# Splitting the contraction of a feed-forward: 128 rows at once, or two halves of 64 rows into two PSUM banks

## The chip, the cores and the metric

The kernel runs on one core of a Trainium2 chip. A core has a matrix engine (TensorE, PE in the profile) that reads both operands from SBUF and writes only to PSUM, three engines for elementwise work (VectorE or DVE, ScalarE or ACT, GpSimd or POOL), and a queue (SyncE or SP) from which this kernel issues its DMAs. PSUM has eight banks; one bank holds 128 partitions of 512 float32 values. The metric is the device time of one execution, in microseconds (us); lower is better. A profiled execution gives a trace of every instruction, and the profile's times count from the first instruction (the span).

## The reference

Block-sparse attention over 4 batches of 8 heads, 768 positions and 64 dimensions, and then a feed-forward over its output:

```python
scores = scale * np.matmul(q, k.transpose(0, 1, 3, 2))
scores = np.where(mask, scores, -1000000000.0)   # own block and its neighbours, first and last block, 3 sampled blocks
attn = np.exp(scores - np.max(scores, axis=-1, keepdims=True))
attn = attn / (np.sum(attn, axis=-1, keepdims=True) + 1e-09)
x = np.matmul(attn, v)            # (4, 8, 768, 64), then transposed to (3072 tokens, 512)
h = x @ w_in                      # (3072, 512) @ (512, 2048)
r = np.maximum(h, 0.0)
g = s * (r * r) + b               # s and b are single numbers
return (g @ w_out).astype(np.float32)   # (3072, 2048) @ (2048, 512)
```

The weights arrive as 64-bit floats. The feed-forward is kept near float32 accuracy by writing each operand as a high and a low part in the fast float32 form of TensorE (`F32R`, fp32r in the profile) and forming three of the four products: high by high, high by low, low by high.

## The kernel before

**Attention** (the first 290 us) works through 'units' of one head pair and 128 query positions. Its instructions are put in order by a planner in the kernel: each operation has an engine, an estimated cost, a due time (priority) and its dependences, and the planner simulates the engines to write an order for each queue. The table `T` holds the due times, among them those of the K loads (`KL`), the query loads (`QL`), the gathers of sampled V blocks (`GV`) and the latency assumed for the weight loads (`LATE`). The attention output goes to DRAM (`xd`) and comes back transposed for the feed-forward.

**Feed-forward.** The 3072 tokens form 8 groups of 384 tokens (`G`), the hidden dimension 16 blocks of 128. A 'sub' is one group and one block, `subs[i] = (g, f)`, 128 subs in all. Groups 0 and 1 come first, interleaved (subs 0 to 31; the planner orders the first 30 of them beside the end of the attention and the decoding of the weights). Groups 2 to 7 follow, one after the other, 16 subs each, 96 subs in all, in the order in which the loop at the end of the kernel writes them. For one sub:

- `mlp1(i)`: 4 chunks of the model dimension by 3 products = 12 matmuls, each a 128x128 weight block against 384 token columns, all summed in one PSUM bank. The banks alternate: `i % 2`.
- `relu(i)` on ACT reads that bank into SBUF, `square(i)` on DVE multiplies by itself and by `s`, `hidden_high(i)` on ACT adds `b` and rounds to the high part, `hidden_low(i)` on POOL takes the difference as the low part.
- `mlp2(i)`: 3 token tiles of 128 by 3 products = 9 matmuls, each 128x128 of the hidden values against 512 output columns, summed over all 16 blocks in one bank per token tile. Groups with even and odd number use different banks (2 to 4, and 5 to 7). At the last block (f = 15) the three banks are copied to SBUF, by ACT, DVE and ACT, and stored.

In the loop, PE's order is `mlp1(i)`, `mlp2(i-2)`, `mlp1(i+1)`, `mlp2(i-1)` and so on, so the elementwise chain of a sub has the time of three blocks of PE work between its first use and its last. Each engine runs its own queue in order and waits only on semaphores.

Attention already has matmuls that use half of the array's rows: `scores_static` (L694) multiplies 64 dimensions of one head, with `tile_position=(0, 0)` for one head and `(64, 0)` for the other, each into its own bank.

Of the kernel before, what the change touches and what calls it, by code (L numbers as in the profile page):

```python
# [14 lines left out]
AF = mybir.ActivationFunctionType  # L15
ALU = mybir.AluOpType
# [3 lines left out]
P = 128  # L20
# [182 lines left out]
def kernel(  # L203
# [176 lines left out]

    def mlp1(i, cs=range(NCC)):
        g, f = subs[i]
        if 0 in cs:
            hid[i] = bank(i % 2, f"h{g}_{f}")[:, :G]
        ph = hid[i]
        for c in cs:
            xh, xl = (xsp[(g, k)][:, c, :] for k in range(2))
            wh, wl = (win(f, k)[:, c * P:(c + 1) * P] for k in range(2))
            nc.tensor.matmul(ph, wh, xh, start=(c == 0), stop=False)  # L389
            nc.tensor.matmul(ph, wh, xl, start=False, stop=False)  # L390
            nc.tensor.matmul(ph, wl, xh, start=False, stop=(c == NCC - 1))  # L391

    def relu(i):
        nc.scalar.activation(htile(i % 2), hid.pop(i), AF.Relu)  # L394

    def square(i):
        t = htile(i % 2)
        nc.vector.scalar_tensor_tensor(out=t, in0=t, scalar=sb_s, in1=t, op0=ALU.mult, op1=ALU.mult)  # L398

    def hidden_high(i):  # L400
        t, gh = htile(i % 2), htile(2 + i % 3)
        nc.scalar.activation(t, t, AF.Identity, bias=sb_b)  # L402
        nc.scalar.copy(gh, t)  # L403
# [11 lines left out]
    def mlp2(i):  # L415
        g, f = subs[i]
        gh, gl = htile(2 + i % 3), htile(5 + i % 3)
        b, hf = divmod(g, 2)
        for t in range(TG):
            if f == 0:  # L420
                po[(g, t)] = bank(2 + 3 * hf + t, f"o{g}_{t}")
            acc = po[(g, t)]
            tsl = slice(t * P, (t + 1) * P)
            nc.tensor.matmul(acc, gh[:, tsl], wout(f, 0), start=(f == 0), stop=False)  # L424
            nc.tensor.matmul(acc, gh[:, tsl], wout(f, 1), start=False, stop=False)  # L425
            nc.tensor.matmul(acc, gl[:, tsl], wout(f, 0), start=False, stop=(f == NFC - 1))  # L426
            if f == NFC - 1:
                ob = wos["pool"].tile([P, DM], F32, tag="ob", name=f"ob{g}_{t}", bufs=3)
                if t % 2 == 0:
                    nc.scalar.copy(ob, acc)  # L430
                else:
                    nc.vector.tensor_copy(ob, acc)
                tok = BLK + hf * G + t * P
                if tok + P <= S:
                    nc.sync.dma_start(out=out[b * S + tok:b * S + tok + P, :], in_=ob)
                else:
                    nc.sync.dma_start(out=out[b * S + tok:(b + 1) * S, :], in_=ob[:P - BLK])
                    nc.sync.dma_start(out=out[b * S:b * S + BLK, :], in_=ob[P - BLK:])
# [4 lines left out]
    with ExitStack() as es:  # L443
# [498 lines left out]
        for i, (kind, b, t, x) in enumerate(slots):  # L942
# [3 lines left out]
            if qk not in lqs:  # L946
                for par in range(2):
                    pq = lqs[qk] = op("s", 450, u - (T["QL"] if i else 50) + 0.1 * par, lambda qk=qk, par=par: load_q(qk, par), alloc=[] if par else [("qr", qk)],
# [99 lines left out]
        for k, (which, f) in enumerate((w[0], int(w[1:])) for w in T["WL"].split()):  # L1048
# [3 lines left out]
            mine = {}  # L1052
            for m, (eng, fn, needs) in enumerate(st):
# [62 lines left out]
    for i in range(NPL, NSUB + LAG):  # L1116
        s = SUB0 + i
        if i < NSUB:
            mlp1(i)
        if i - LAG >= NPL - 1:  # L1120
            mlp2(i - LAG)
        if i < NSUB:
            relu(i)
# [86 lines left out]
```

## Time and profile before

| | |
|---|---|
| time, median of 3 runs | 828.12 us (822.63 to 832.83) |
| profiled execution | 827.27 us, its span 825.5 us |
| PE busy | 803.8 us of the span, 97% |
| PE's granted clock, mean | 0.993 |
| ACT, DVE, POOL busy | 57%, 49%, 25% |

The table of the profile's first part gives each engine's busy time. 'PEld' is the loading of weights into the array, which has its own record for every matmul. A PE record lasts from its start to a modelled end that includes the pipeline's latency, so consecutive records overlap: what a matmul costs in a dense stream is the distance from one start to the next, not its duration. The timeline gives the start and length in microseconds, then engine, line, operation, what is written and read, and the shape (weights first for a matmul, as rows*columns, then the moving operand).

### The profile page before, as it was taken

The numbers are of one execution on the slowest core, as the hardware profiler recorded it, in microseconds if no ns is written. First come the engines' busy times: TensorE is split into PE (matmuls) and PEld (weight loads), VectorE is DVE, ScalarE is ACT, GpSimd is POOL, SyncE is SP. The second block draws the span as 40 slices with busy tenths as digits, with TensorE's granted clock in tenths as the row PEclk, the third lists the DMA queues.
The fourth block names the chain that finished last, engine by engine and source line by source line (L and its number), as shares of the span: only waits on it lengthen the run. The fifth ranks groups of instructions, "written<-read, shape, count | busy, mean of one in ns | idle before, by whom it ended". The sixth has DMA issues, their size and how long they took to land.

```text
span 825.5 us, 21605 instructions
## 1 busy us (share of the span) xinstructions
PE 803.8 (97%) x8512; PEld 699.8 (85%) x8512; DVE 408.0 (49%) x1061; ACT 472.9 (57%) x1107; POOL 206.8 (25%) x436
## 2 busy tenths in 40 slices
PE   7889999999999999999999999999999999999998
PEld 5677877888876889999989999999999999999996
DVE  4666778888987899999631221212212112122111
ACT  3666768878886788778554434434434444444433
POOL 1722133222300032222222222222222222222221
PEclk9999999999999999999999999999999999999999
DMA  8997897877777423433130010002002002001001
GB/s 253 271 234 279 225 254 199 246 234 226 213 198 225 142 102 102 129 107 123 39 115 1 1 66 11 1 1 77 0 1 77 1 1 77 0 1 39 1 1 38
DMA packets 79061, 89.03 MB, mean 108 GB/s; under 512 B 10736, under 2 KB 57968, under 8 KB 78960
## 3 DMA queue, kind: packets, MB, share of 16 engines
q1 hardware_dynamic: 78960, 87.66, 36.3%
q8 instruction: 67, 1.10, 0.6%
q14 instruction: 34, 0.28, 0.1%
HBM read 75.05 MB, written 12.58 MB: 106 GB/s over the span
## 4 chain that ended last, share of the span: by engine, by line
PE 88%; DMA 4%; SPq 3%; issue 2%; DVE 1%; ACT 1%; POOL 0%; DVEq 0%; POOLq 0%; ACTq 0%
PE o L425 11%; PE o L426 11%; PE o L424 11%; PE h L391 10%; PE h L389 10%; PE h L390 10%; PE t L771 8%; PE xs L816 5%; PE s L694 4%; PE xs L830 3%; PE s L720 2%; DMA kt<-in_k_seq_dram 2%; PE s L708 1%; DMA vg<-in_v_dram 1%; SPq L637 1%
## 5 line engine op out<-in xcount | busy, mean ns | idle before, releaser
L407 POOL TENSOR_TENSOR hid<-hid,hid 128x384 fp32r<-128x384 f32 x128 | 135.2, 1057 | 465.9 <-ACT hid L403 456.4
L398 DVE SCALAR_TENSOR_TENSOR hid<-hid,sb_s 128x384 f32<-128x384 f32 x128 | 83.3, 652 | 306.0 <-ACT hid L394 305.8
L389 PE MATMUL h<-x,win 128*128 128x384 f32 x512 | 172.7, 337 | 0.6 <-ACT hid L394 0.6
L391 PE MATMUL h<-x,win 128*128 128x384 f32 x512 | 172.7, 337 | 0.0
L390 PE MATMUL h<-x,win 128*128 128x384 f32 x512 | 172.1, 336 | 0.2 <-DVE x L363 0.2
L394 ACT ACTIVATE hid<-h 128x384 f32<-128x384 f32 x128 | 62.7, 490 | 153.7 <-PE h L391 152.1
L747 ACT ACTIVATE ptile<-ptile,nm 128x352 f32<-128x352 f32 (+2 forms) x208 | 120.8, 583 | 32.5 <-DVE nm L735 31.6
L402 ACT ACTIVATE hid<-hid,sb_b 128x384 f32<-128x384 f32 x128 | 78.8, 616 | 72.9 <-DVE hid L398 72.9
L389 PEld LDWEIGHTS h<-x,win 128*128 128x128 f32 x512 | 96.2, 188 | 6.5 <-ACT hid L394 0.9
L390 PEld LDWEIGHTS h<-x,win 128*128 128x128 f32 x512 | 96.1, 188 | 5.8 <-DVE x L363 0.6
L391 PEld LDWEIGHTS h<-x,win 128*128 128x128 f32 x512 | 96.0, 188 | 0.0
L654 POOL COPY kg<-kt 128x128 f32 x264 | 63.6, 293 | 128.0 <-PE s L720 123.9
L735 DVE CUSTOM_DVE_ANT_0 ptile<-s,ms 128x352 f32<-128x352 f32 x160 | 74.4, 521 | 27.3 <-PE s L720 27.0
L771 PE MATMUL t<-ident,ptile 128*128 128x128 f32 x608 | 79.7, 280 | 1.7 <-DVE nm L735 0.9
L426 PE MATMUL o<-wout,hid 128*128 128x512 f32 x192 | 75.9, 395 | 0.0
L426 PE MATMUL o<-woutr,hid 128*128 128x512 f32 x192 | 75.9, 395 | 0.0
L425 PE MATMUL o<-wout,hid 128*128 128x512 f32 x192 | 75.8, 395 | 0.0
L425 PE MATMUL o<-woutr,hid 128*128 128x512 f32 x192 | 75.8, 395 | 0.0
L424 PE MATMUL o<-wout,hid 128*128 128x512 f32 x192 | 74.7, 389 | 0.0
L424 PE MATMUL o<-woutr,hid 128*128 128x512 f32 x192 | 74.6, 389 | 0.0
L771 PEld LDWEIGHTS t<-ident,ptile 128*128 128x128 f32 x608 | 66.5, 142 | 7.9 <-ACT ptile L747 2.2
L403 ACT CAST hid<-hid 128x384 fp32r<-128x384 f32 x128 | 65.8, 514 | 4.4 <-PE o L425 0.4
(131 smaller groups left out, 1080.8 us busy)
## 6 DMA issues: line engine op xcount, KB each, us to landing
vg<-in_v_dram SPq DMA_DIRECT2D x136, 128.0 KB, 3.7
v<-in_v_sta_dram SPq DMA_DIRECT2D x40, 256.0 KB, 4.3
kt<-in_k_seq_dram SPq DMA_DIRECT2D x16, 544.0 KB, 7.3
raw_i<-in_w_in_dram SPq DMA_DIRECT2D x16, 512.0 KB, 4.0
raw_o<-in_w_out_dram SPq DMA_DIRECT2D x16, 512.0 KB, 3.2
v<-in_v_dram SPq DMA_DIRECT2D x16, 384.0 KB, 6.1
xd<-xst SPq DMA_DIRECT2D x44, 128.0 KB, 3.9
xraw<-xd SPq DMA_DIRECT2D x14, 384.0 KB, 4.1
```

Of the source, the lines that this page charges most:

```text
L389: nc.tensor.matmul(ph, wh, xh, start=(c == 0), stop=False)
L390: nc.tensor.matmul(ph, wh, xl, start=False, stop=False)
L391: nc.tensor.matmul(ph, wl, xh, start=False, stop=(c == NCC - 1))
L398: nc.vector.scalar_tensor_tensor(out=t, in0=t, scalar=sb_s, in1=t, op0=ALU.mult, op1=ALU.mult)
L402: nc.scalar.activation(t, t, AF.Identity, bias=sb_b)
L407: nc.gpsimd.tensor_tensor(out=htile(5 + i % 3), in0=t, in1=gh.bitcast(F32), op=ALU.subtract)
L424: nc.tensor.matmul(acc, gh[:, tsl], wout(f, 0), start=(f == 0), stop=False)
L425: nc.tensor.matmul(acc, gh[:, tsl], wout(f, 1), start=False, stop=False)
L426: nc.tensor.matmul(acc, gl[:, tsl], wout(f, 0), start=False, stop=(f == NFC - 1))
L735: nc.vector.tensor_tensor_reduce(out=pt[:, :w], in0=sps.pop((n, g))[:, :w], in1=msk, scale=-scale, scalar=FMAX if g == 0 else nm[:, 0:1], ...
L747: nc.scalar.activation(pt[:, :w], pt[:, :w], AF.Exp, bias=nms[n][:, last:last + 1], scale=-1.0, accum_out=dns[i][:, g, j:j + 1])
L771: nc.tensor.transpose(tp[:, c, :], src[:, c * P:(c + 1) * P], ident)
```

## The change

From group 2 on (`in_halves`), each matmul of `mlp1` and `mlp2` becomes two: rows 0 to 63 of both operands at tile position (0, 0) into one bank, rows 64 to 127 at (64, 0) into another. `mlp1` now fills banks 0 and 1 for every sub in place of alternating; `mlp2` holds six banks (2 to 7) for the three token tiles of a group, in place of three banks and the other three for the next group. The two sums of a hidden tile are added on the way out: ACT copies the first bank, DVE adds the second, and then DVE squares with the maximum against zero inside (`scalar=0.0`, `ALU.max`), while `s` moves into ACT's scale. The output tiles are also copied by ACT and added to by DVE. `relu(i)` is written ahead of `mlp2(i-2)` in the loop, for all subs. Subs 0 to 31 keep whole products.

In the planner's table four due times change, the first query load takes the common due time, and the load of group 0's tokens is ordered behind that of weight block i7. Instructions of PE and POOL in the attention keep their order.

```diff
-    "GK": 9.0, "GV": [7.0, 15.0, 15.0, 15.0, 15.0, 15.0], "KL": [46.0, 18.0, 26.0, 26.0], "QL": 18.0, "VL": 10.0, "SI": 31.8, "MS1": -23.3, "MS2": -1.6,
+    "GK": 9.0, "GV": [9.0, 15.0, 15.0, 15.0, 15.0, 15.0], "KL": [26.0, 18.0, 26.0, 26.0], "QL": 18.0, "VL": 10.0, "SI": 31.8, "MS1": -23.3, "MS2": -1.6,
...
+    row_halves = [slice(0, P // 2), slice(P // 2, P)]
+    def in_halves(i):
+        return subs[i][0] >= 2
+    def products(to, pairs, first, last):
+        for k, (w, x) in enumerate(pairs):
+            start, stop = first and k == 0, last and k == len(pairs) - 1
+            if len(to) == 1:
+                nc.tensor.matmul(to[0], w, x, start=start, stop=stop)
+            else:
+                for rows, o in zip(row_halves, to):
+                    nc.tensor.matmul(o, w[rows], x[rows], start=start, stop=stop, tile_position=(rows.start, 0))
     def mlp1(i, cs=range(NCC)):
-            hid[i] = bank(i % 2, f"h{g}_{f}")[:, :G]
+            hid[i] = [bank(k, f"h{g}_{f}_{k}")[:, :G] for k in ((0, 1) if in_halves(i) else (i % 2,))]
...
-            nc.tensor.matmul(ph, wh, xh, start=(c == 0), stop=False)
-            nc.tensor.matmul(ph, wh, xl, start=False, stop=False)
-            nc.tensor.matmul(ph, wl, xh, start=False, stop=(c == NCC - 1))
+            products(hid[i], [(wh, xh), (wh, xl), (wl, xh)], c == 0, c == NCC - 1)
     def relu(i):
-        nc.scalar.activation(htile(i % 2), hid.pop(i), AF.Relu)
+        h = hid.pop(i)
+        if in_halves(i):
+            t = htile(i % 2)
+            nc.scalar.copy(t, h[0])
+            nc.vector.tensor_tensor(out=t, in0=h[1], in1=t, op=ALU.add)
+        else:
+            nc.scalar.activation(htile(i % 2), h[0], AF.Relu)
     def square(i):
+        if in_halves(i):
+            nc.vector.scalar_tensor_tensor(out=t, in0=t, scalar=0.0, in1=t, op0=ALU.max, op1=ALU.mult)
     def hidden_high(i):
-        nc.scalar.activation(t, t, AF.Identity, bias=sb_b)
+        nc.scalar.activation(t, t, AF.Identity, bias=sb_b, scale=sb_s if in_halves(i) else 1.0)
     def mlp2(i):
-                po[(g, t)] = bank(2 + 3 * hf + t, f"o{g}_{t}")
+                po[(g, t)] = [bank(k, f"o{g}_{t}_{k}") for k in ((2 + 2 * t, 3 + 2 * t) if in_halves(i) else (2 + 3 * hf + t,))]
...
+                if in_halves(i):
+                    nc.scalar.copy(ob, acc[0])
+                    nc.vector.tensor_tensor(out=ob, in0=acc[1], in1=ob, op=ALU.add)
...
-                    pq = lqs[qk] = op("s", 450, u - (T["QL"] if i else 50) + 0.1 * par, lambda qk=qk, par=par: load_q(qk, par), alloc=[] if par else [("qr", qk)],
+                    pq = lqs[qk] = op("s", 450, u - T["QL"] + 0.1 * par, lambda qk=qk, par=par: load_q(qk, par), alloc=[] if par else [("qr", qk)],
...
+            if which == "i" and f == 7:
+                for c2 in range(2):
+                    xl[(0, c2)].order.append(pw)
...
             mlp1(i)
+            relu(i)
         if i - LAG >= NPL - 1:
             mlp2(i - LAG)
-        if i < NSUB:
-            relu(i)
```

PE's queue before, at the end of a sub's `mlp2` and the start of the next `mlp1` in group 3 (`o3_2` is the bank of group 3's third token tile, `h3_11` that of hidden block 11; `hid` are hidden values, `x3_0` and `x3_1` the high and low parts of the tokens, `win` and `woutr` weights):

```order
L424 MATMUL o3_2_8741<-woutr_7562,hid4_7125 128x512
L425 MATMUL o3_2_8741<-woutr_7562,hid4_7125 128x512
L426 MATMUL o3_2_8741<-woutr_7562,hid7_7139 128x512
L389 MATMUL h3_11_8978<-x3_0_8455,win2_7437 128x384
L390 MATMUL h3_11_8978<-x3_1_8457,win2_7437 128x384
L391 MATMUL h3_11_8978<-x3_0_8455,win2_7437 128x384
```

Three products of the tile are followed by the first three products of the next hidden block.

PE's queue in the changed kernel, at the same place (the last number before the buffer's own is the bank):

```order
L395 MATMUL o3_2_6_9166<-woutr_7596,hid7_7125 128x512
L395 MATMUL o3_2_7_9167<-woutr_7596,hid7_7125 128x512
L395 MATMUL h3_11_0_9590<-x3_0_8647,win2_7462 128x384
L395 MATMUL h3_11_1_9591<-x3_0_8647,win2_7462 128x384
L395 MATMUL h3_11_0_9590<-x3_1_8649,win2_7462 128x384
L395 MATMUL h3_11_1_9591<-x3_1_8649,win2_7462 128x384
L395 MATMUL h3_11_0_9590<-x3_0_8647,win2_7462 128x384
L395 MATMUL h3_11_1_9591<-x3_0_8647,win2_7462 128x384
```

Every row has become two neighbours that differ in the bank alone (`_0` and `_1`, `_6` and `_7`); the rows of one product stand next to each other.

DVE's queue before, where group 4's output is copied out while group 5 has begun (`hid0`, `hid1` are the two buffers of hidden values, `ob4_1` the copy of group 4's second token tile):

```order
L398 SCALAR_TENSOR_TENSOR hid1_7088<-hid1_7088,sb_s_62 128x384
L398 SCALAR_TENSOR_TENSOR hid0_7051<-hid0_7051,sb_s_62 128x384
L432 COPY ob4_1_9623<-o4_1_9196 128x512
L398 SCALAR_TENSOR_TENSOR hid1_7088<-hid1_7088,sb_s_62 128x384
L398 SCALAR_TENSOR_TENSOR hid0_7051<-hid0_7051,sb_s_62 128x384
```

DVE has one square per sub, and one of the group's three output copies.

DVE's queue in the changed kernel, at the same place (`h5_1_1` is the second bank of group 5's hidden block 1):

```order
L411 TENSOR_TENSOR hid0_7061<-h5_0_1_10676,hid0_7061 128x384
L418 SCALAR_TENSOR_TENSOR hid0_7061<-hid0_7061 128x384
L411 TENSOR_TENSOR hid1_7080<-h5_1_1_10726,hid1_7080 128x384
L451 TENSOR_TENSOR ob4_0_10759<-o4_0_3_9984,ob4_0_10759 128x512
L451 TENSOR_TENSOR ob4_1_10769<-o4_1_5_9992,ob4_1_10769 128x512
L451 TENSOR_TENSOR ob4_2_10779<-o4_2_7_10000,ob4_2_10779 128x512
L418 SCALAR_TENSOR_TENSOR hid1_7080<-hid1_7080 128x384
L411 TENSOR_TENSOR hid0_7061<-h5_2_1_10788,hid0_7061 128x384
```

Each square has an addition ahead of it, and three output additions stand between the addition and the square of block 1.

SP's queue at the start of the kernel before (`qr0_5d` is the first query tile, `kt0` and `kt1` the keys of batches 0 and 1, `sbi` the sampled block numbers):

```order
L484 DMA qr0_5d_160<-in_q_edge_dram 64x4x128 x2
L474 DMA kt0_168<-in_k_seq_dram 128x1088 x4
L534 DMA sbi_177<-in_sampled_dram 128x144
L474 DMA kt1_179<-in_k_seq_dram 128x1088
L484 DMA qr1_5d_181<-in_q_edge_dram 64x4x128 x2
```

SP's queue at the start of the changed kernel:

```order
L557 DMA sbi_160<-in_sampled_dram 128x144
L497 DMA kt0_162<-in_k_seq_dram 128x1088 x3
L507 DMA qr0_5d_171<-in_q_edge_dram 64x4x128 x2
L497 DMA kt0_162<-in_k_seq_dram 128x1088
L497 DMA kt1_183<-in_k_seq_dram 128x1088
L507 DMA qr1_5d_187<-in_q_edge_dram 64x4x128 x2
```

The block numbers have moved to the front, and the first query tile behind three of the four key loads. Further on, the first V gather stands ahead of the first store to `xd` in place of behind it.

More of the change, by code (lines that the diff above doesn't have):

```diff
@@ L383, in mlp1 @@
         if 0 in cs:
-            hid[i] = bank(i % 2, f"h{g}_{f}")[:, :G]
-        ph = hid[i]
+            hid[i] = [bank(k, f"h{g}_{f}_{k}")[:, :G] for k in ((0, 1) if in_halves(i) else (i % 2,))]
         for c in cs:
@@ L388, in mlp1 @@
             wh, wl = (win(f, k)[:, c * P:(c + 1) * P] for k in range(2))
-            nc.tensor.matmul(ph, wh, xh, start=(c == 0), stop=False)
-            nc.tensor.matmul(ph, wh, xl, start=False, stop=False)
-            nc.tensor.matmul(ph, wl, xh, start=False, stop=(c == NCC - 1))
+            products(hid[i], [(wh, xh), (wh, xl), (wl, xh)], c == 0, c == NCC - 1)
     def relu(i):
-        nc.scalar.activation(htile(i % 2), hid.pop(i), AF.Relu)
+        h = hid.pop(i)
[5 more added lines that the diff above has]
+            nc.scalar.activation(htile(i % 2), h[0], AF.Relu)
     def square(i):
         t = htile(i % 2)
-        nc.vector.scalar_tensor_tensor(out=t, in0=t, scalar=sb_s, in1=t, op0=ALU.mult, op1=ALU.mult)
+        if in_halves(i):
+            nc.vector.scalar_tensor_tensor(out=t, in0=t, scalar=0.0, in1=t, op0=ALU.max, op1=ALU.mult)
+        else:
+            nc.vector.scalar_tensor_tensor(out=t, in0=t, scalar=sb_s, in1=t, op0=ALU.mult, op1=ALU.mult)
     def hidden_high(i):
         t, gh = htile(i % 2), htile(2 + i % 3)
-        nc.scalar.activation(t, t, AF.Identity, bias=sb_b)
+        nc.scalar.activation(t, t, AF.Identity, bias=sb_b, scale=sb_s if in_halves(i) else 1.0)
         nc.scalar.copy(gh, t)
@@ L420, in mlp2 @@
             if f == 0:
-                po[(g, t)] = bank(2 + 3 * hf + t, f"o{g}_{t}")
+                po[(g, t)] = [bank(k, f"o{g}_{t}_{k}") for k in ((2 + 2 * t, 3 + 2 * t) if in_halves(i) else (2 + 3 * hf + t,))]
             acc = po[(g, t)]
             tsl = slice(t * P, (t + 1) * P)
-            nc.tensor.matmul(acc, gh[:, tsl], wout(f, 0), start=(f == 0), stop=False)
-            nc.tensor.matmul(acc, gh[:, tsl], wout(f, 1), start=False, stop=False)
-            nc.tensor.matmul(acc, gl[:, tsl], wout(f, 0), start=False, stop=(f == NFC - 1))
+            products(acc, [(gh[:, tsl], wout(f, 0)), (gh[:, tsl], wout(f, 1)), (gl[:, tsl], wout(f, 0))], f == 0, f == NFC - 1)
             if f == NFC - 1:
                 ob = wos["pool"].tile([P, DM], F32, tag="ob", name=f"ob{g}_{t}", bufs=3)
-                if t % 2 == 0:
-                    nc.scalar.copy(ob, acc)
+                if in_halves(i):
+                    nc.scalar.copy(ob, acc[0])
+                    nc.vector.tensor_tensor(out=ob, in0=acc[1], in1=ob, op=ALU.add)
+                elif t % 2 == 0:
+                    nc.scalar.copy(ob, acc[0])
                 else:
-                    nc.vector.tensor_copy(ob, acc)
+                    nc.vector.tensor_copy(ob, acc[0])
                 tok = BLK + hf * G + t * P
```

2 rows, old and new, of the table T are left out of this document.

## The prediction

> **What bounds the kernel now.** I read the page first, then stretches of 50 us, then single instructions.
>
> ```profile
> span 825.5 us, 21605 instructions
> PE 803.8 (97%) x8512; PEld 699.8 (85%) x8512; DVE 408.0 (49%) x1061; ACT 472.9 (57%) x1107; POOL 206.8 (25%) x436
> ...
> PE 88%; DMA 4%; SPq 3%; issue 2%; DVE 1%; ACT 1%; POOL 0%; DVEq 0%; POOLq 0%; ACTq 0%
> ```
>
> PE is busy for 97% of the span and makes 88% of the chain that ended last. The stretches say where it is alone (columns: length, busy time of PE, PEld, DVE, ACT, POOL, PE's granted clock, DMA share, GB/s).
>
> ```profile
> 0.00:50.00 50.00, 40.54 (x567) 30.12 (x568) 27.47 (x105) 25.48 (x75) 22.29 (x104) 0.96 0.97 260
> ...
> 550.00:600.00 50.00, 50.00 (x253) 45.29 (x252) 10.50 (x17) 21.95 (x42) 12.17 (x12) 1.00 0.10 32
> ```
>
> In the stretch of the changed subs PE never stops, at full clock, while DVE works a fifth of the time and ACT less than half. So only what a product costs on PE, or a new stop of PE, can move the time. One sub of the changed stretch:
>
> ```profile
> 601.68 0.39 PE L424 MATMUL o<-woutr,hid 128*128 128x512 f32 x1
> ...
> 603.76 0.33 PE L389 MATMUL h<-x,win 128*128 128x384 f32 x1
> ```
>
> ```profile
> 601.94 0.49 ACT L394 ACTIVATE hid<-h 128x384 f32<-128x384 f32 x1 [1.85 <-PE h L391]
> 602.47 0.62 DVE L398 SCALAR_TENSOR_TENSOR hid<-hid,sb_s 128x384 f32<-128x384 f32 x1 [3.10 <-ACT hid L394]
> 603.12 0.62 ACT L402 ACTIVATE hid<-hid,sb_b 128x384 f32<-128x384 f32 x1 [0.69 <-DVE hid L398]
> 603.77 0.51 ACT L403 CAST hid<-hid 128x384 fp32r<-128x384 f32 x1
> 604.41 1.02 POOL L407 TENSOR_TENSOR hid<-hid,hid 128x384 fp32r<-128x384 f32 x1 [3.17 <-ACT hid L403]
> 606.13 0.49 ACT L394 ACTIVATE hid<-h 128x384 f32<-128x384 f32 x1 [1.85 <-PE h L391]
> ```
>
> A sub takes 4.19 us (601.94 to 606.13): 2.08 for the nine products of `mlp2` (601.68 to 603.76), 2.11 for the twelve of `mlp1`. The chain from the end of `mlp1` to the low part ends at 605.43, while `mlp2` of that sub starts two subs later, near 610: it is covered by over 4 us.
>
> What is in a product? Two dense runs of one kind give its parts, before and after the mixed stretch.
>
> ```profile
> 290.72 0.33 PE L389 MATMUL h<-x,win 128*128 128x384 f32 x1
> ...
> 293.84 0.33 PE L389 MATMUL h<-x,win 128*128 128x384 f32 x1
> ...
> 817.51 0.39 PE L425 MATMUL o<-woutr,hid 128*128 128x512 f32 x1
> ...
> 820.91 0.39 PE L425 MATMUL o<-woutr,hid 128*128 128x512 f32 x1
> 821.14 0.39 PE L426 MATMUL o<-woutr,hid 128*128 128x512 f32 x1
> ```
>
> From 290.72 to 293.84 there are 18 steps: 3.12 / 18 = 0.1733 us for 384 columns. From 817.51 to 820.91 there are 15: 3.40 / 15 = 0.2267 us for 512. The difference, 0.0533 over 128 columns, is 0.417 ns per column, and what is left is fixed: 0.1733 - 384 x 0.417 ns = 13.3 ns for each product. This fixed part is 12 x 13.3 + 9 x 13.3 = 0.28 us of a sub; the rest of the 4.19 is 3.84 of streaming and 0.07 where the two kinds follow each other.
>
> **The change part by part.**
>
> *Products in halves.* A half streams as many columns as the whole product, so the pair costs one product only if the halves run side by side, and it gains only if the fixed part shrinks. The attention already has such pairs, in plain float32, 64 rows by 256 columns, each product in two passes; they run here between 154.69 and 155.82.
>
> ```profile
> 154.69 0.49 PE L694 MATMUL s<-kt,qr_0s 64*128 64x256 f32 x2
> 154.69 1.13 PE L694 MATMUL s<-kt,qr_0s 64*128 64x256 f32 x8
> L694 PE MATMUL s<-kt,qr_0s x8: 376/376/480, 154.7 to 155.5; 64*128 64x256 f32 x8
> L694 PEld LDWEIGHTS s<-kt,qr_0s x2: 183/183/183, 154.7 to 154.7; 64*128 64x128 f32 x2
> ```
>
> The first two records (x2) last 480 ns each and 0.49 us together, so both halves run at once, and so do their two weight loads, which start together at 154.7. The first pair has 104 ns of exposed load (480 against 376). The last pair starts 1.13 - 0.376 = 0.754 after the first, so three steps of a pair take 0.754 - 0.104 = 0.65, 0.217 us each. If such a pass streams a column in two of the steps found above, 256 columns take 0.213, and the pair's fixed part is 3 ns. So side by side is shown, and at this slower rate the fixed part is almost nothing. What these rows do not show is whether the fixed part is small because of the halves or because of the rate.
>
> I take the rate. The fixed part lies inside the record of a product: 0.334 - 0.160 = 0.174 us beside its columns, against 0.376 - 0.213 = 0.163 for the half-row pass. And the row at 821.14 is the kernel's last matmul; no load follows it, yet it lasts 0.39 as the others do. So it isn't the next load that stretches it, and each half streams the same columns through its own rows, with a load of its own. I put the pair at the whole product's price: 0 us for 96 subs. The bounds are 96 x 21 x (13.3 - 3) = -20.8 us, with the 0.07 at the joints -27.5 us, and the other way 13.3 ns more per pair, +26.8 us.
>
> *Additions.* DVE gets one addition per sub. Its nearest rows are the subtraction and the square, and for the output the copy:
>
> ```profile
> L398 DVE SCALAR_TENSOR_TENSOR hid<-hid,sb_s 128x384 f32<-128x384 f32 x96 | 62.6, 652 | 296.4 <-ACT hid L394 296.4
> L363 DVE TENSOR_TENSOR x<-xraw,x 128x384 fp32r<-128x384 f32 x20 | 11.0, 552 | 0.0
> L432 DVE COPY ob<-o 128x512 f32<-128x512 f32 x7 | 4.8, 691 | 28.6 <-PE o L426 26.1 <-DMA out_dram<-ob 2.5
> ```
>
> I take 0.62 for 384 elements (0.55 to 0.65) and 0.70 for 512 (0.69 to 0.76). In an ordinary sub this lies beside PE: 96 x 0.62 us on an engine that is 80% idle. The chain grows from 3.5 to 4.15 us and keeps over 3 us of cover. New is that banks 0 and 1 serve every sub: `mlp1(i+1)` waits for the addition of sub i, done 0.26 + 0.49 + 0.04 + 0.62 = 1.41 us after `mlp1(i)`; it starts after 2.08. Cover 0.67 us, cost nothing.
>
> *Group ends.* Here the cover goes. Behind the addition of sub (g+1, 1) DVE's queue holds three output additions, and behind them the square.
>
> ```profile
> 489.54 0.59 ACT L430 COPY ob<-o 128x512 f32<-128x512 f32 x1 [2.48 <-PE o L426]
> 490.92 0.59 ACT L430 COPY ob<-o 128x512 f32<-128x512 f32 x1 [0.80 <-PE o L426]
> ```
>
> Count from the end of `mlp1`, when `mlp2` begins; tile 0's third product starts 2 x 0.23 after that, lasts 0.39 and can be copied from 0.90 on; tile 2 follows 1.38 later (489.54, 490.92), tile 1 midway. ACT copies to 1.49, 2.18, 2.87; DVE adds to 2.23, 2.93, 3.63, squares to 4.25; ACT's two steps end at 5.44, and only then comes its copy of the next sub, to 5.96, and DVE's addition to 6.62. PE wants bank 1 at 4.19 + 2.08 = 6.27. It stops 0.4 us, at 5 group ends: +2.0 us (3.0 with the slower additions).
>
> *Tail.* The last output tile is copied and then added to: +0.04 + 0.70 = +0.74 us. The last low part, 0.66 later, is ready at 819.6, just ahead of its first use near 819.8; at a faster PE it would cost some tenths.
>
> *Attention.* The sampled numbers move ahead, the first query tile behind more key loads.
>
> ```profile
> 10.33 2.80 PE L708 MATMUL s<-kt,qr_5d 64*64 64x384 f32 x28
> ...
> 49.32 1.03 PE L830 MATMUL xs<-vg,pt 96*32 96x64 f32 x26 [2.18 <-DMA vg<-in_v_dram]
> ...
> kt<-in_k_seq_dram SPq DMA_DIRECT2D x16, 544.0 KB, 7.3
> ```
>
> Earlier gathers can end the wait of 2.18 us at 49.32. Against it, PE's first scores at 10.33 need the query tile, and that tile now has one key load (544 KB) ahead of it that these scores don't read; at 260 GB/s, the rate of the first stretch, that is 2.1 us. I take 0, with -2.2 and +2.1 as ends.
>
> Sum against the profiled execution: 827.27 + 0 + 2.0 + 0.74 + 0 = 830.0 us. That execution lies 0.85 us under the median of the runs shown, less than they spread (822.63 to 832.83). What a measurement of this kernel can tell from no change is about 2%: below 811.6 or above 844.7.
>
> **The rivals.**
>
> *The fixed part goes.* A load for one half could run under the other half, and the fixed part fall to the 3 ns of the attention's pairs. For it: the pair rows above. Against it: loads ride under whole products already.
>
> ```profile
> 601.16 0.33 PE L389 MATMUL h<-x,win 128*128 128x384 f32 x1
> ...
> 601.16 0.19 PEld L390 LDWEIGHTS h<-x,win 128*128 128x128 f32 x1
> ```
>
> The load for the next product starts with this one, in the same rows of the array. The Trainium skill, "TensorE: Matmul & The Clock Gate", Part 3 (packing small matmuls), says that a weight load overlaps a running matmul only where the row groups differ; by that rule whole products pay for loads that halves hide. The trace disagrees with its letter, since the loads are recorded inside the products; by it the 13.3 ns would be the unhidden rest. Time: a pair costs 0.163 and 0.216, the sub 12 x 0.163 + 9 x 0.216 = 3.90, so 96 x -0.29 = -27.8 us. The group ends then cost 0.8 each (PE wants bank 1 at 5.85), 4 us, and the tail 1 us: 804.5 us. Chance 0.28.
>
> *The fixed parts add.* Each half brings its own 13.3 ns, and one stands in the way of the other, since both leave one queue in order. For it: PE issues twice the instructions. Against it: in the 3 ns of the attention's pair there is no room for this. Place: every pair of the 96 subs; price 13.3 ns x 21 x 96 = 26.8 us; it decides, by passing 2%, from (844.7 - 830.0) / (96 x 21) = 7 ns more per pair. The slower PE hides the group ends: 827.27 + 26.8 + 0.74 = 855 us. Chance 0.17.
>
> *The halves don't run side by side.* At the fast rate a pair would hand over two columns for each one of the whole product, which no row here shows. If halves follow each other, each sub costs another 4.1 us: about 1220 us. If only the loads do, a pair of 384 waits for 2 x 104 ns: 12 x (0.208 - 0.174) x 96 = 39 us, 868 us. Together 0.09. The Trainium skill, "TensorE: Matmul & The Clock Gate", in its table of why this matters, says that a product of few rows takes as long as one of all rows and the gain lies in running tiles together; it also gives 3.07 for four such tiles. By that figure, 0.77 a tile, I estimate two halves at 1.3 products, near 950 us; no run here shows it.
>
> **How the numbers follow.** Forecast 0.46 (820 to 840 us), fixed part gone 0.28, fixed parts added 0.17, one after the other 0.09. Range: down to 800, the first rival with the gain of the attention; up to 858, the second with its loss; that leaves out the last rival and the edges. Faster by over 2%: 0.28, and 0.01 of the forecast's edge; slower: 0.17 + 0.09, with 0.01 of that edge; within 2%: 0.44.
>
> **What would show it.** Two records of one product start within 0.01 us, and from pair to pair it is 0.173 to 0.185 for 384 columns and 0.227 to 0.236 for 512: then the pair has the old price. Near 0.163 and 0.216 the first rival is right, with means above 0.183 and 0.238 (now 0.176 and 0.231) the second; a second half that starts after the first half's columns shows the third. ACT's copies at the same distance as before, 4.19 us, is the sum of it. PE's wait for DVE at five group ends, some 0.4 us each, shows the queue on DVE; none there, and the walk was wrong. The wait on `vg` near 49 and PE's first scores show the attention's part.

## The result, and the profile after

The changed kernel takes 838.72 us (median of 4, 833.08 to 841.07), beside 830.31 us for the kernel before on the same chip (median of 4, 822.63 to 832.83): a ratio of 1.0124, with a 95% interval of 1.0079 to 1.0169. It is slower by 10 us, within the 2% and inside the range. The profiled execution takes 838.24 us against a forecast of 830.0, so 8 us are unaccounted for. The ratios leave out slow executions, among them one of 978.51 us of the planner's part alone and one of 1971.61 us of the halves alone, which the medians include. The page of the changed kernel, first its span, the engines' busy time and the chain that ended last:

```profile
span 836.5 us, 25875 instructions
PE 809.4 (97%) x10528; PEld 733.9 (88%) x10528; DVE 458.7 (55%) x1169; ACT 485.4 (58%) x1113; POOL 206.9 (25%) x436
...
PE 87%; DVE 4%; DMA 3%; SPq 2%; ACT 2%; issue 1%; ACTq 0%; DVEq 0%
```

PE is busy 5.6 us longer, with a span 11 us longer: so part of the loss is PE standing still, and part is PE working more slowly. DVE works 50.7 us more and is still at 55%. The stretches of the changed kernel (the same columns as before: length, busy PE, PEld, DVE, ACT, POOL, granted clock, DMA share, GB/s):

```profile
0.00:50.00 50.00, 42.05 (x571) 32.14 (x572) 27.55 (x106) 24.81 (x74) 22.59 (x104) 0.90 0.93 248
240.00:260.00 20.00, 14.94 (x276) 12.73 (x267) 11.19 (x38) 11.43 (x35) 0.00 (x0) 0.83 0.63 183
248.60:252.00 3.40, 3.40 (x67) 3.11 (x68) 0.42 (x3) 3.16 (x10) 0.00 (x0) 0.50 0.27 48
412.00:416.00 4.00, 2.02 (x5) 1.42 (x6) 3.71 (x7) 1.28 (x4) 0.08 (x1) 0.83 0.59 195
416.00:420.00 4.00, 4.00 (x17) 3.52 (x17) 1.81 (x3) 0.70 (x2) 0.00 (x0) 0.74 0.01 4
550.00:600.00 50.00, 50.00 (x506) 49.86 (x504) 15.66 (x28) 22.47 (x41) 12.20 (x12) 1.00 0.10 33
```

The last row is the stretch that the change rewrote, and nothing is wrong there: PE full, clock full, twice the instructions (506, or 253 pairs, where 253 products stood before). The damage is in rows 2 to 5, near 245 and 415 us, in work that the halves don't touch. What PE waited for there, by its waits (total, times, longest) and then by the timeline (in brackets the idle time before an instruction, and what ended it):

```profile
PE xs L839 <- ACT xst L870: 5.1, 1, 5.1
...
PE o L392 <- DVE woutr L83: 1.7, 1, 1.7
...
PE s L731 <- DMA qr_5d<-in_q_edge_dram: 1.1, 1, 1.1
```

```profile
245.25 0.93 ACT L361 CAST x<-xraw 128x384 fp32r<-128x384 f32 x2 [6.82 <-DMA xraw<-xd]
248.58 1.98 PE L839 MATMUL xs<-v,pt 128*64 128x64 f32 x32 [5.07 <-ACT xst L870]
...
413.29 0.49 PE L392 MATMUL o<-woutr,hid 128*128 128x512 f32 x1 [1.71 <-DVE woutr L83]
414.47 3.63 PE L392 MATMUL o<-woutr,hid 128*128 128x512 f32 x8 [0.69 <-DVE woutr L85]
```

Near 243 us ACT stands for 6.82 us at the splitting of group 0's tokens, whose load is now ordered behind weight block i7 (it goes out at 240.13 us, where in the kernel before it went out at 197.78 and the splitting at 223.51 found it done); behind it in ACT's queue are the copies that PE's next matmuls need, and PE stops for 5.07 us. Near 412 us PE waits 1.71 and 0.69 us for an output weight that DVE has decoded too late. With both stops the clock falls: it is granted 0.50 over 3.4 us from 248.6 on, and 0.74 from 416 to 420.

A table of where each feed-forward product starts shows when the time is lost. It counts the 2688 products in order (a pair of halves is one), and gives the changed kernel's start less that of the kernel before, in us, from the two traces:

| place | product | after - before | gained or lost since the row above |
|---|---|---|---|
| first product of the feed-forward (286.39 and 282.34) | 0 | +4.05 | +4.05 |
| inside groups 0 and 1 | 200 | +4.83 | +0.78 |
| just ahead of the waits for the late weight | 600 | +4.83 | 0 |
| after them | 640 | +9.38 | +4.55 |
| passage from whole to half products | 714 | +10.12 | +0.74 |
| five group ends later | 2600 | +10.24 | +0.12 |
| last product | 2687 | +10.28 | +0.04 |
| end of the span (836.5 and 825.5) | | +11.0 | +0.7 |

Of the 11 us, 9.4 are lost before the first half product has run. The first row compares two single executions, and some 3 us of it belong to the execution and not to the edits (see the attention, in the part on why the prediction was right or wrong).

### The profile page after: what moved, and what is told of

It is laid out like the page before. It is cut to its first block, busy times and chain, and to the rows that moved or that the text cites. A ratio compares the mean times of both kernels' runs of the same rounds, so it can differ in the third digit from the quotient of the medians.

```text
span 836.5 us, 25875 instructions
## 1 busy us (share of the span) xinstructions
PE 809.4 (97%) x10528; PEld 733.9 (88%) x10528; DVE 458.7 (55%) x1169; ACT 485.4 (58%) x1113; POOL 206.9 (25%) x436
## 4 chain that ended last, share of the span: by engine, by line
PE 87%; DVE 4%; DMA 3%; SPq 2%; ACT 2%; issue 1%; ACTq 0%; DVEq 0%
PE o L395 24%; PE h L395 24%; PE t L794 8%; PE o L392 7%; PE h L392 6%; PE xs L839 5%; PE s L717 4%; PE xs L853 3%; PE s L743 2%; DMA kt<-in_k_seq_dram 2%; PE xs L828 1%; PE s L731 1%; PE xs L865 1%; SPq L660 1%; DMA vg<-in_v_dram 1%
## 5 line engine op out<-in xcount | busy, mean ns | idle before, releaser
L395 PE MATMUL h<-x,win 64*128 64x384 f32 x2304 | 230.9, 334 | 0.0
L395 PEld LDWEIGHTS h<-x,win 64*128 64x128 f32 x2304 | 219.9, 184 | 3.5 <-issue 0.7
L424 ACT ACTIVATE hid<-hid,sb_b,sb_s 128x384 f32<-128x384 f32 x96 | 68.0, 709 | 106.4 <-DVE hid L418 106.4
L395 PE MATMUL o<-wout,hid 64*128 64x512 f32 x864 | 114.1, 390 | 0.0
L395 PE MATMUL o<-woutr,hid 64*128 64x512 f32 x864 | 113.5, 390 | 0.0
L395 PEld LDWEIGHTS o<-woutr,hid 64*128 64x128 f32 x864 | 98.9, 184 | 2.5
L395 PEld LDWEIGHTS o<-wout,hid 64*128 64x128 f32 x864 | 98.6, 184 | 2.8
L392 PE MATMUL h<-x,win 128*128 128x384 f32 x384 | 72.3, 338 | 0.0
L392 PEld LDWEIGHTS h<-x,win 128*128 128x128 f32 x384 | 68.0, 189 | 2.7 <-DVE x L363 0.2
L798 DVE COPY pt<-t 128x384 f32<-128x384 f32 (+1 forms) x104 | 56.5, 546 | 12.8 <-PE t L794 10.7
```

Source lines behind the costliest of these rows:

```text
L392: nc.tensor.matmul(to[0], w, x, start=start, stop=stop)
L395: nc.tensor.matmul(o, w[rows], x[rows], start=start, stop=stop, tile_position=(rows.start, 0))
L424: nc.scalar.activation(t, t, AF.Identity, bias=sb_b, scale=sb_s if in_halves(i) else 1.0)
L798: nc.vector.tensor_copy(to, src)
```

## The experiments

The first question was whether the halves or the planner's five edits (three due times at the start, `LATE`, the order of the token load) cost the time. "Theory 1" in the first expectations is that the planner's edits do; from the second set on, "theory 2" names what followed from it. The intervals below are at 95%, and the us in brackets are the ratio's interval times the median of the kernel before.

**The planner's part alone.** The kernel before, whole products throughout, with the change's edits to the planner:

```diff
-"LATE": 3000.0  GV[0] 7.0  KL[0] 46.0
+"LATE": 5000.0  GV[0] 9.0  KL[0] 26.0
-u - (T["QL"] if i else 50) + 0.1 * par
+u - T["QL"] + 0.1 * par
+            if which == "i" and f == 7:
+                for c2 in range(2):
+                    xl[(0, c2)].order.append(pw)
```

> The kernel before with only the planner's part of the change: LATE 5000, first GV 9, first KL 26, the common due time for the first query load, and group 0's token load ordered behind weight block i7. Whole products throughout. Theory 1 (the time that was lost comes from the planner's part): 836 to 840 us, first matmul of the feed-forward some 4 us later than before, and a second loss of 4 to 5 us between 400 and 430 us. Rival (it comes from the halves, with their additions and the earlier reading of the first bank): 827 to 831 us, as before.

Measured 833.26 us, ratio 1.0073 (1.0038 to 1.0109): +6.0 us (3.1 to 9.0), under the 836 to 840 us that theory 1 expected of it. Both stops are there (4.9 us for `xst`, 1.7 and 0.7 for the late weight), but its attention was otherwise shorter: its first feed-forward product starts 0.93 us after that of the kernel before, and not 4.05.

**The halves alone.** The changed kernel with the diff above taken back.

> The changed kernel with the planner's part taken back: halves, additions and the earlier relu alone. Theory 1: 829 to 831 us, 1 us above before (0.6 us at the end for the additions, a few tenths at group ends). Rival (the halves cost the time): 836 to 840 us.

828.43 us, ratio 1.0006 (0.9972 to 1.004). The halves, their additions, the shared banks and the moved `relu` together make no difference that can be measured. In its trace the halves cost 0.73 us at the passage and 0.19 at the group ends, near the changed kernel's 0.74 and 0.16, and 0.6 at the end: 1.5 us, which the interval does not rule out (-2.3 to +3.3 us).

**The price of a product.** The prediction took the fixed 13.3 ns of a product to stay with halves; the Trainium skill's rule and the attention's pairs spoke for the other way. The kernel before, with dense runs added at its end that nothing interrupts (24 products each, 12 in plain float32); its time thus holds some 60 us of added work (two of the ten runs are shown; the comments say what each is):

```diff
+    for k in range(24):
+        nc.tensor.matmul(Q[0], fr[k % 2][:, :P], fr[k % 2], start=True, stop=True)          # L1148, F32R, 128 rows
...
+        for j in range(2):
+            nc.tensor.matmul(Q[j], fr[k % 2][H[j], :P], fr[k % 2][H[j]], start=True, stop=True, tile_position=(64 * j, 0))   # L1158
```

> The kernel before, with ten dense runs of matmuls behind its last one, each 24 or 12 products long, which cost extra time at the end only and whose sums nobody reads: fast float32 in whole rows with 512 and with 256 columns, with 64 in place of 128 weight columns, in quarters of 32 rows, in halves, in one half alone; plain float32 whole and in halves; bfloat16 whole and in halves. Theory A (the fixed 13.3 ns belongs to each product in the fast float32 form, whatever rows it has, and halves merely run two such chains side by side): 0.227 us from product to product for 512 columns in whole rows, in halves, in quarters and for a half alone; 0.120 for 256; plain float32 near 0.429 a pass, whole as in halves; bfloat16 near 0.216. Theory B (it belongs to any product at one column a step): bfloat16 at 0.227 too. Theory C (it is the weight load's, and grows with its columns): 0.220 with 64 weight columns, the others as in A.

The timeline of this kernel's PE, one row for each run (start, length of the whole run, number of records):

```profile
824.30 5.60 PE L1148 MATMUL bench<-woutr 128*128 128x512 f32 x24
829.74 3.03 PE L1150 MATMUL bench<-woutr 128*128 128x256 f32 x24
832.61 5.68 PE L1152 MATMUL bench<-woutr 128*64 128x512 f32 x24
838.22 5.77 PE L1155 MATMUL bench<-woutr 32*128 32x512 f32 x96
843.92 5.74 PE L1158 MATMUL bench<-woutr 64*128 64x512 f32 x48
849.50 5.60 PE L1160 MATMUL bench<-woutr 64*128 64x512 f32 x24
855.03 10.57 PE L1162 MATMUL bench<-woutr 128*128 128x512 f32 x24
865.52 10.57 PE L1165 MATMUL bench<-woutr 64*128 64x512 f32 x48
876.25 5.13 PE L1167 MATMUL bench<-benchw 128*128 128x512 bf16 x23 [0.16 <-issue]
881.31 5.35 PE L1170 MATMUL bench<-benchw 64*128 64x512 bf16 x48
```

A run's length less one record (0.39 us in F32R, 0.60 in plain float32, 0.38 in bf16, 0.28 for 256 columns), over its steps, is the price. F32R: whole 5.21 / 23 = 0.227 us; one half alone the same (L1160); pairs of halves 0.233 and quarters 0.234, and without their first step (0.335 and 0.340 us from the first start to the second) 0.228 as well. 64 in place of 128 weight columns (L1152): 0.230, no cheaper. 256 columns: 2.75 / 23 = 0.120. Plain float32, two passes and records a product: 0.434 a pass with the first step, 0.429 by the starts of the others, whole or halved, so 2 x 213.3 + 2.6 ns. bf16: 4.75 / 22 (one record is missing) = 0.216 whole, 0.216 halved, 2.5 ns over its columns. Theory B falls with the bf16 runs, and theory C with the 64 weight columns. Theory A holds: the 13.3 ns belong to the F32R product, whatever rows it uses, and the 3 ns of the attention's pairs belong to plain float32 and not to halves. The Trainium skill, "TensorE: Matmul & The Clock Gate", Part 1 ("Wait — 56ns, not 53.3ns?"), gives about 2.5 ns over the columns for a bf16 matmul at full clock; the bf16 runs here agree (215.8 ns, 2.5), and F32R pays five times that. The rule of Part 3 of the same page of the Trainium skill that was weighed in the prediction, loads overlap only where row groups differ, would have made halves cheaper: they take 0.228 against 0.227.

**`LATE` and the order without the start's numbers.**

```diff
-"LATE": 3000.0
+"LATE": 5000.0
+            if which == "i" and f == 7:
+                for c2 in range(2):
+                    xl[(0, c2)].order.append(pw)
```

> The kernel before with two pieces of the planner's part that bear on the weights: LATE 5000 and group 0's token load behind weight block i7. Theory 1a (these two make the stops near 243 and 411 us, where ACT waits for the tokens and PE for late weights): 833 to 838 us with a wait of some 5 us of PE near 243. Rival 1b (the order at the start makes the difference, by shifting what comes later): 827 to 831 us, and no such wait.

837.26 us, ratio 1.0113 (1.0054 to 1.0173): +9.4 us (4.5 to 14.3). PE's wait near 243 is 5.6 us, its first feed-forward product comes 4.70 us late, and the waits for the weight add 4.5: these two edits alone give the whole loss, and the three others must gain. That gave the next set, one edit each.

**The start's numbers alone** (`GV[0]`, `KL[0]`, the first query load):

```diff
-GV[0] 7.0  KL[0] 46.0   u - (T["QL"] if i else 50) + 0.1 * par
+GV[0] 9.0  KL[0] 26.0   u - T["QL"] + 0.1 * par
```

> The kernel before with three of the planner's changes alone: the gather's due time GV[0] 9, the key load's KL[0] 26, and the first query load on the common due time. Theory 2 (the planner's part is three pieces that add up): these numbers save 3 to 3.6 us of the attention by 100 us, as in the two runs that had them (the changed kernel -3.15, the planner's part alone -3.57), nothing stops PE near 243 or 411 us, and the gain stays to the end: 1 to 4 us under the kernel before. Rival 2b (the gain is lost again, since the end of the attention waits for transfers that don't come earlier): PE is ahead at 100 us and level again at the first feed-forward product, no difference.

820.97 us, ratio 0.9957 (0.9924 to 0.999): -3.6 us (-6.3 to -0.8), faster than both kernels. By its windows PE is busy for 43.37 us of the first 50, where it was 40.54:

```profile
0.00:50.00 50.00, 43.37 (x579) 33.15 (x580) 28.52 (x107) 25.39 (x76) 22.42 (x104) 0.90 0.93 250
```

The wait for `vg` near 49 us is gone, and PE is 3.9 us ahead near 71 us. It stays ahead, by 3.3 us near 237 us and by 6.2 at the first feed-forward product of this execution: rival 2b falls. A single trace says little here, since the attention varies from one execution to the next; but near 86 us PE is 2.7 to 3.6 us ahead in all five traces with the start's numbers, and in the six others it lies between 1.5 us ahead of the kernel before and 3.0 behind it.

**`LATE` alone.**

> The kernel before with LATE 5000 alone. Theory 2: no wait near 243; DVE takes hidden squares ahead of pieces of the last output weight's decoding, and near 411 us PE waits 1.7 and 0.7 us for that weight and then goes at half clock for a while: +4 to +5 us in all. Rival 2a (the late decoding comes from the order of the token load, which also moves DVE's and ACT's queues): within 1 us of the kernel before, no wait for the weight.

831.09 us, ratio 1.005 (1.0015 to 1.0084): +4.1 us (1.2 to 6.9). Nothing at 243, and in PE's timeline the two waits for the weight:

```profile
405.79 0.50 PE L424 MATMUL o<-woutr,hid 128*128 128x512 f32 x1 [1.70 <-DVE woutr L83]
406.98 0.50 PE L425 MATMUL o<-woutr,hid 128*128 128x512 f32 x1 [0.69 <-DVE woutr L85]
```

`LATE` moves no load (SP's queue is that of the kernel before, row by row); it changes the order of the weights' decoding on DVE and ACT, among itself and against the hidden squares. In DVE's timeline here a `win` block is finished (402.57 to 405.13) ahead of the `woutr` that PE waits for:

```profile
402.57 0.69 DVE L83 TENSOR_TENSOR win<-wkhp,raw_i 128x512 fp32r<-128x512 f32 x1
...
405.06 0.68 DVE L83 TENSOR_TENSOR woutr<-wkhp,raw_o 128x512 fp32r<-128x512 f32 x1
```

The kernel before finishes two `woutr` in a row there (398.60 and 401.62), with a hidden square between them. In this execution no slow clock followed the stop, and it cost 2.97 us; with one, in the three other traces that have it, 4.4 to 4.6.

**The order of the token load alone.**

> The kernel before with group 0's token load behind weight block i7 alone. Theory 2: PE stops for 5 to 6 us near 243 because ACT's queue stands at the splitting of the tokens, the first feed-forward product is 4 to 5 us later, and nothing is lost near 411: +4 to +5 us in all. Rival 2a: the same stop near 243 and the waits for the last output weight near 411 as well: +9 to +10 us.

831.93 us, ratio 1.0078 (1.004 to 1.0116): +6.4 us (3.3 to 9.6), over the 4 to 5 expected, though its trace has the last product only 4.1 us later than that of the kernel before; a stop of 6.30 us near 243, and no wait for the weight:

```profile
245.70 0.92 ACT L361 CAST x<-xraw 128x384 fp32r<-128x384 f32 x2 [8.05 <-DMA xraw<-xd]
249.03 1.98 PE L816 MATMUL xs<-v,pt 128*64 128x64 f32 x32 [6.30 <-ACT xst L847]
```

So each stop has its own edit, and rival 2a falls. The three pieces add up: -3.6 + 4.1 + 6.4 = +6.9 us, beside 6.0 measured for all of them.

**The halves with the start's numbers, without the other two edits.**

> The changed kernel without LATE 5000 and without the order of the token load: halves and the start's three numbers. Theory 2: both stops gone, 9 us less than the changed kernel, 0 to 3 us under the kernel before (the start's gain less 0.7 us at the passage from whole to half products and 0.6 at the end). Rival 2b: 1 to 2 us over the kernel before.

824.65 us, ratio 0.9983 (0.9951 to 1.0016), 0.9983 / 1.0124 = 0.986 of the changed kernel. Its profiled execution takes 821.96 us, beside 821.07 for the same start with whole products; the halves gain nothing there either. The start's gain is smaller here than alone, 1.4 us (-4.0 to +1.3 us against the kernel before), which the interval does not tell from none.

**The group ends.** The prediction's walk gave PE a stop of 0.4 us at each, and the trace has 0.01 to 0.04. Is the walk wrong, or only its durations? The kernel of the last experiment, with each output addition done twice:

```diff
+                    nc.vector.tensor_tensor(out=spare[0], in0=acc[1], in1=ob, op=ALU.add)
                     nc.vector.tensor_tensor(out=ob, in0=acc[1], in1=ob, op=ALU.add)
```

> The kernel of e8_halves_and_start, with each output addition on DVE done twice (once into a spare tile, once as before), so that three more additions of 0.69 us stand in DVE's queue at each of the five group ends, and at the end of the kernel. Theory 3 (the walk of the prediction is right and only its durations were too long: with 0.56 for the hidden addition and the square in place of 0.62 the group end just fits, with nothing to spare): PE now stops 3 x 0.69 = 2.07 us at each of the five group ends, 10 us in all, and some us more if the clock falls after the stops; the tail is 0.7 longer. Rival 3b (DVE's queue doesn't limit the group ends, other slack takes it up): the blocks of mlp1 after the group ends stay within 0.3 us of 2.106, and only the tail grows.

842.49 us in one run; the five group ends make up 10 us of its distance to the kernel that it was made from, and the rest lies in the attention of this execution (first feed-forward product at 284.04 us, there at 275.35). One of its group ends, on its timeline (DVE, ACT and PE together, in order of time):

```profile
564.26 2.40 PE L396 MATMUL o<-wout,hid 64*128 64x512 f32 x18
...
564.96 0.69 DVE L455 TENSOR_TENSOR ob<-o,ob 128x512 f32<-128x512 f32 x1
565.56 0.55 DVE L419 SCALAR_TENSOR_TENSOR hid<-hid 128x384 f32<-128x384 f32 x1
...
567.30 0.47 ACT L411 COPY hid<-h 128x384 f32<-128x384 f32 x1
...
567.83 0.44 PE L396 MATMUL h<-x,win 64*128 64x384 f32 x1 [1.17 <-ACT hid L411]
568.42 2.37 PE L396 MATMUL h<-x,win 64*128 64x384 f32 x23 [0.15 <-DVE hid L412]
570.46 2.41 PE L396 MATMUL o<-wout,hid 64*128 64x512 f32 x18
```

The chain is the one that the walk named: third output addition, square, ACT's two steps, ACT's copy, DVE's addition, and PE waits first for the copy (bank 0), then for the addition (bank 1). From 564.26 to 570.46 are 6.20 us, where the two blocks take 4.19: PE loses 2.01 us at each of the five ends. The prolongation is 3 x 0.69 = 2.07; so without it the walk just fits, with less than 0.1 us to spare.

**Changing between whole products and halves.** Where the changed kernel passes from whole to half products, `mlp1` is already halved while `mlp2` still is not, and a sub takes longer than its two blocks of 2.08 and 2.11 us. On its timeline, two starts of `mlp2` one sub apart:

```profile
426.92 2.34 PE L392 MATMUL o<-woutr,hid 128*128 128x512 f32 x9
...
431.49 2.34 PE L392 MATMUL o<-woutr,hid 128*128 128x512 f32 x9
```

From 426.92 to 431.49 are 4.57 us in place of 4.19. The kernel before, with runs added at its end in which the forms take turns (some 80 us of added work; the comment stands for two more loops):

```diff
+    for n in (1, 4):
+        for c in range(12):
+            for k in range(n):
+                whole(k)
+            for k in range(n):
+                pair(k)
+    # then 12 x (four whole, four of one half alone), 12 x (four of one half alone, four pairs)
```

> The kernel before, with products of 512 columns added at its end that take turns: 12 times one whole product and one pair of halves; 12 times four of each; 12 times four whole ones and four of one half alone; 12 times four of one half alone and four pairs. No other engine works there and no product waits for a semaphore between them. Theory 4 (changing between 128 rows and 64 rows costs PE about 0.2 us each time, since the load for the other form does not run under the product; that is the +0.7 us where the changed kernel passes from whole to half products): a cycle takes 0.453 + 0.4 = 0.87 us, 1.813 + 0.4 = 2.2 us, 2.2 us, and 1.8 us for the last, where both kinds use 64 rows. Rival 4b (the +0.7 came from waits for ACT and DVE, which share the banks there): 0.45, 1.81, 1.81 and 1.81 us.

On PE's timeline (L1148 whole, L1152 pairs, L1155 one half alone):

```profile
826.53 0.50 PE L1148 MATMUL bench<-woutr 128*128 128x512 f32 x1
...
827.40 0.50 PE L1148 MATMUL bench<-woutr 128*128 128x512 f32 x1
...
839.03 1.21 PE L1148 MATMUL bench<-woutr 128*128 128x512 f32 x4
...
841.30 1.19 PE L1148 MATMUL bench<-woutr 128*128 128x512 f32 x4
...
862.72 1.19 PE L1155 MATMUL bench<-woutr 64*128 64x512 f32 x4
...
864.97 1.19 PE L1155 MATMUL bench<-woutr 64*128 64x512 f32 x4
...
892.05 1.17 PE L1152 MATMUL bench<-woutr 64*128 64x512 f32 x6
...
893.86 1.17 PE L1152 MATMUL bench<-woutr 64*128 64x512 f32 x6
```

Cycles take 0.87 us (826.53 to 827.40), 2.257 on average (839.03 to 841.30 is one), 2.25 (862.72 to 864.97), and 1.814 for one half against pairs (892.05 to 893.86). Theory 4 holds: (2.257 - 1.814) / 2 = 0.22 us for each change of form, with no other engine at work. By the starts, the last product ahead of a change takes 0.32 us and the first behind it 0.33, each 0.1 longer than 0.227: that is the size of the exposed first load of a pair in the prediction's rows (0.104). The records of the weight loads show it: inside a run the load for the next product starts with the product ahead of it (both at 839.62), and the first load after a change starts only with its own product (both at 840.18).

## Why the prediction was right or wrong

The time lies inside the range, and that is partly luck: the range was drawn from the rivals about the halves. The forecast was +2.7 us; what came, +10.3 us, is another sum, with terms of the planner's edits that the prediction put at 0 or did not have.

*The halves* were put at 0 us for 96 subs, by taking the rate and not the halves as the reason for the attention's small fixed part. The size was right, and so was it that the halves aren't the reason. The rate isn't either: the bf16 runs take 512 columns in 0.216 us, a column a step as F32R does, and their fixed part is 2.5 ns. What the 13.3 ns go with is the F32R form. ACT's copies in the changed stretch stand 4.18 us apart:

```profile
603.74 0.48 ACT L410 COPY hid<-h 128x384 f32<-128x384 f32 x1 [1.23 <-POOL hid L429]
...
607.92 0.48 ACT L410 COPY hid<-h 128x384 f32<-128x384 f32 x1 [1.23 <-POOL hid L429]
```

In ordinary subs the blocks take 2.106 and 2.081 us, as before. The rivals that let the fixed part go, double it, or run the halves one after the other are out, in the kernel and in the added runs, and so is the estimate of 1.3 products for two halves: dense pairs take 0.228 us where a whole product takes 0.227. One sign given for it was wrong: the two records of a product don't start within 0.01 us of each other in steady state. In the trace they stand 54 to 170 ns apart (600.1 to 603.5 us), as if each half of the rows ran its own chain at the whole product's pace.

*The additions* in ordinary subs cost nothing, as forecast. Their durations, in the page's groups of the changed kernel (busy us, mean ns):

```profile
L411 DVE TENSOR_TENSOR hid<-h,hid 128x384 f32<-128x384 f32 x96 | 53.6, 558 | 268.6 <-ACT hid L410 268.6
L424 ACT ACTIVATE hid<-hid,sb_b,sb_s 128x384 f32<-128x384 f32 x96 | 68.0, 709 | 106.4 <-DVE hid L418 106.4
...
L418 DVE SCALAR_TENSOR_TENSOR hid<-hid 128x384 f32<-128x384 f32 x96 | 53.5, 558 | 3.1
```

*The group ends* are the mis-sized term: +2.0 us forecast, 0.16 measured. The mechanism was right, as the doubled additions show. The step that failed is "I take 0.62 for 384 elements": the addition takes 0.56, and so does the square, which I kept at its old 0.62 although the edit takes its tensor scalar away. That is 0.13 of the 0.30 us by which the walk came out too long. Most of the rest is a second step: the walk put records end to end, and in the trace the square, and ACT's copy, each start 0.09 us before the record ahead of them ends. ACT's scaling is dearer, 0.71, and takes 0.1 back. In the trace (the start of `mlp2` on PE, then DVE, ACT's copy, DVE and PE):

```profile
565.79 0.39 PE L395 MATMUL o<-woutr,hid 64*128 64x512 f32 x1
...
569.29 0.55 DVE L418 SCALAR_TENSOR_TENSOR hid<-hid 128x384 f32<-128x384 f32 x1
...
571.04 0.47 ACT L410 COPY hid<-h 128x384 f32<-128x384 f32 x1
...
571.55 0.56 DVE L411 TENSOR_TENSOR hid<-h,hid 128x384 f32<-128x384 f32 x1 [1.71 <-ACT hid L410]
572.06 2.45 PE L395 MATMUL h<-x,win 64*128 64x384 f32 x24
```

The addition ends at 572.11; `mlp2` began at 565.79, so it is done after 6.32 us and not 6.62, against PE's want at 6.27.

*The tail* was +0.74, and is +0.7.

*The passage* had no term: whole and half products alternate there, and I looked only at dense runs of one form. It costs 0.74 us: of its five changes of form, four cost 0.19 each over an ordinary joint, and the first falls into a wait of PE that the kernel before has at the same product (a step of 0.52 us there, 0.43 here).

*The attention* is where the prediction failed. Its step reads "I take 0, with -2.2 and +2.1 as ends", and it weighed only the start. There it was right about both ends, the `vg` wait goes and PE's first scores wait 1.11 us for the query tile, but too small in size: the start's numbers gain 3.6 us. Wholly missing are the other two edits. The order of the token load stood in the part on the change; `LATE` was there only as one of its "four due times", without its row (three entries of the table change: `GV`, `KL` and `LATE`). I gave neither a term, since PE's and POOL's queues in the attention kept their order: ACT's token splitting and DVE's decoding didn't, nor, with the token load, did SP. The token load behind i7 costs 6.4 us (3.3 to 9.6), `LATE` 4.1 (1.2 to 6.9). Near 243 us the kernel before has ACT idle for less than 0.4 us at a time, so a stop of 6.8 us in that queue finds no slack; that could have been read from its trace.

The distance of the changed kernel (+10.3 us, 6.6 to 14.0) from the sum of its pieces (+6.9 for the planner's, +0.5 for the halves) is within the intervals. The attention itself varies: with the loads of the kernel before in the same order, the first feed-forward product starts at 279.67 to 285.28 us in five traces. The changed kernel reached it 3.1 us later than the kernel with the same planner edits, and the traces show where: it loses 3.3 us against that kernel between 136 and 178 us. Near 139 us PE waits 0.69 and 1.50 us for a gathered V block, and from 141.6 to 145.0 the clock is 0.50; in the other trace the same wait is 0.75 us, and the clock stays at 1.00. Waits of 2.4 to 2.8 us in all for that block, with a half clock behind them, stand also in the traces of the halves alone, of the price of a product and of the doubled additions, and not in that of the kernel before: this loss goes with the execution and not with an edit. Why the block comes late in some executions is open.

The version that the experiments point to is the kernel before with the start's numbers alone: 820.97 us, 0.43% (0.1 to 0.8) under the kernel before and 1.65% under the changed one (0.9957 / 1.0124).

## What to carry to other kernels

A large rewrite that costs next to nothing (here 0.7 us at the passage, 0.2 at the group ends and 0.7 at the end) can come with small edits that do: give every edit a term, tables of numbers included, and for a load that is ordered later, follow the in-order queue of each engine that uses it, not only the matmuls' order. A step of a dense stream of matmuls that lies in the instruction's form (here the F32R product's 13.3 ns) isn't won by splitting its rows; measure it by one dense run of each form. Stay in one form of tile: each change between 128 and 64 rows cost 0.22 us here. And compare one execution with one other only where they can differ by the edit alone: in this attention, traces with the same loads spread over 5.6 us.

## What the runs showed of the hardware that was not expected

- A matmul in F32R pays 13.3 ns over its columns, whether it uses 128, 64 or 32 rows; bf16 pays 2.5 and plain float32 2.6 for a pass, which takes two steps a column (0.227, 0.216 and 0.429 us for 512 columns).
- A change between whole and half products adds about 0.1 us on either side of it, 0.22 us in all; a change between one half alone and pairs of halves costs nothing (1.814 us a cycle).
- A short stop of PE can cost more than its length: with the stop of 5.07 us the clock was 0.50 for 6.83 us, from 247.42 on, before the stop had ended; the same wait of 1.7 and 0.7 us cost 2.97 us without a slow stretch behind it and 4.4 to 4.6 with one. The Trainium skill, "TensorE: Matmul & The Clock Gate", Part 1, describes a free-running window of about 3.4 us after which an idle array falls to half rate. The rate and the lengths here agree: in the changed kernel's trace the clock changes at 247.42, 254.25, 414.68 and 418.09 us, which are 2, 47 and 1 times 3.413 us apart. But PE need not be idle for a whole window: counted on this grid, 2.40 us of idle time in the window up to 414.68 brought the next one to half rate, and 1.65 us in the window that held most of the wait in the run with `LATE` alone did not.
- The square without a tensor scalar, and with a maximum in place of a product, takes 558 ns instead of 619 (medians of groups 2 to 7; the 652 of the prediction's row is a mean that a few long records raise), and ACT's step with a scale from a tensor 709 instead of 616. The Trainium skill, "ScalarE: Activation LUTs" (What ACT_TABLE_LOAD costs), gives about 93 ns for each operand of one value per partition; 709 - 616 = 93 agrees.
